# Seven-product multiplication inside eight of twelve units of a first product, fp16 operands, and a new order of the last products

## The chip, the cores and the metric

The kernel runs on one core of a Trainium2 chip. The core has five engines, each with its own queue of instructions: TensorE (PE, matrix products into PSUM), VectorE (DVE), ScalarE (ACT), GpSimd (POOL) and SyncE (SP, which here only issues transfers). The metric is the device time of one execution in microseconds. All times of the kernel before are three runs: 339.69, 339.77 and 337.69 us.

## The reference

```python
# q, k, v: (batch 8, heads 8, seq 576, head_dim 64); blocks of 64 positions
scores = scale * np.matmul(q, k.transpose(0, 1, 3, 2))
scores = np.where(block_i >= block_j, scores, -1000000000.0)      # causal by block
attn = softmax(scores)                                             # rows
x = np.matmul(attn, v)                    # -> (4608 rows, 512)
h = x @ w_in                              # (512, 2048)
g = h * (1.0 / (1.0 + np.exp(-beta * h)))
out = g @ w_out                           # (2048, 512)
```

Inputs and the output are float32. The kernel computes the swish as g = 0.5 h (1 + tanh(beta h / 2)); the 0.5 is applied where the output leaves PSUM.

## The kernel before

The attention goes over 32 pairs of heads (four per batch entry). Its result is written, turned, into xT, a ring of 2560 rows in SBUF. The two products of the feed-forward part go over nine chunks of 512 rows. A chunk's **first product** has 16 groups j of 128 features. A group is four products on PE (line 971, 512 columns each, contraction 4 x 128) into one PSUM bank, a tanh on ACT (line 981) that reads the bank, and a gate on DVE (line 985) that multiplies the bank by 1 + tanh into gT in fp16, after which the bank is free.

A chunk's **second product** (function `fast`, chunks 1 to 8) is already done by Strassen's seven products over halves of the rows, of the 2048 features and of the 512 outputs, in Winograd's form. Its combinations of gT are made on DVE by `comb` (line 856, two halves for each of four sums, partly in place in gT and partly in the spare tensor OV), those of w_out by `weights` (line 836). `prod` issues each of the seven products as two halves of eight matmuls with 256 columns (line 892). `evac` takes the banks out: on ACT without an addend (line 913), on DVE with one (line 916), `half` for half a bank (line 907), and `store` issues the output transfer (line 923), on ACT's queue, in the last chunk on SP's.

While the attention lasts, POOL casts the loaded Q, K and V (lines 657 and 568) into QKn and Vn, and SP issues loads and the transposes by transfer (lines 664 and 774). Banks 0 to 3 of PSUM belong to the attention's pairs of banks until the last pair has been given out; single banks come from 4 to 7 till then, and from all eight afterwards.

The order of every engine's instructions is fixed when the kernel is built. The class `Plan` holds all operations with a planned duration, dependences, buffers and a priority, and gives each engine, whenever it is free in planned time, the ready operation with the lowest priority number. On PE the first product's group j of chunk r has 1000 + 100 r + j, and the second product's halves get a place between the next chunk's groups. Planned durations are `mm(n)` for a matmul of n columns, `act_t` and `dve_t` for ACT and DVE:

```python
def mm(n):
    return max(n / 2.4 + 3, 55.0)
def act_t(n, ptr=0):
    return 0.833 * n + 93 + 93 * ptr
def dve_t(n):
    return (n + 125) / 0.96
```

The engines then follow their lists with semaphores; nothing in the plan stands for one engine's holding up of another at the SBUF.

Of the kernel before, what the change touches and what calls it, by code (L numbers as in the profile page):

```python
# [13 lines left out]
NF = 2048  # L14
# [17 lines left out]
class Op:  # L32
    def __init__(self, engs, dur, lat, emit, deps, tiles, prio, mode, dma, xfer):
        self.xfer = xfer
        self.engs, self.dur, self.lat, self.emit = engs, dur, lat, emit
        self.deps, self.tiles, self.prio, self.mode, self.dma = list(deps), tiles, prio, mode, dma
        self.eng = None
        self.start = self.end = None
        self.order = None
        self.need = False  # L40
        self.tick = None
        self.after = None
        self.lazy = False
        self.rest = 0.0
        self.pkt = 22.0
        self.fill = 0


class Plan:
# [35 lines left out]
    def schedule(self):  # L85
# [85 lines left out]
        while nsched < len(self.ops) - len(fill) or pend or rings["H"] or rings["S"] or late:  # L171
# [26 lines left out]
            while progress:  # L198
                progress = False
                for e in engs:  # L200
# [60 lines left out]
                    if e == "PE" and start < self.COLD:  # L261
                        o.lat += o.dur
                        o.dur *= 2
                    o.eng, o.start, o.end = e, start, start + o.lat
# [95 lines left out]
def bass_blockwise_causal_attn__then__act_swish_beta_kernel(  # L360
# [10 lines left out]
    with es:  # L371
# [10 lines left out]
        FAST = range(1, NRC)  # L382
        RX = 5 * RC
# [9 lines left out]
        QKn = [sb(f"QKn{i}", [128, 2, 2, 768], bf16) for i in range(NQ)]  # L393
        Vn = [sb(f"Vn{i}", [128, 5, 8, 66], bf16) for i in range(NQ)]
        QKT = [sb(f"QKT{i}", [128, 2, 2, 640], bf16) for i in range(3)]
        Ef = [sb(f"E{i}", [128, 3200], bf16) for i in range(NE)]
        gT = [sb(f"gT{i}", [128, NJ, RC], f16) for i in range(2)]

# [4 lines left out]
        xq = [sb(f"xq{i}", [128, 5, 128], bf16) for i in range(3)]  # L403
        xT = sb("xT", [128, 4, RX], bf16)
        identF = sb("identF", [128, 128], f32)
        identB = sb("identB", [128, 128], bf16)
        w_in = sb("w_in", [128, 4, NF], bf16)
# [7 lines left out]
        PSb = PS[:].rearrange("p b n -> p (b n)").bitcast(bf16).rearrange("p (b n) -> p b n", b=8)  # L415

        identW = identF[:].bitcast(bf16)
# [5 lines left out]
        P.slots("S4", 4)  # L423

# [105 lines left out]
        for b in range(B):  # L530
            ts, t = P.tile("Vs"), P.tile("V")
            ts.only = (b,) if b < 2 else (0,)
            early += [ts] * (b < 2)
            tl[b] = t
            for h0, h1, e, tt in PARTS[b]:

                vs = []
                for i in tt:
                    def fv(g, e, ts=ts, t=t, b=b, h0=h0, h1=h1, i=i):
                        d = Vn[t.slot] if e == "POOL" else Vs[ts.slot]  # L540
                        if i < 4:
                            return [g.dma_start(d[:, i, h0:h1, 0:64],
                                                v[b, h0:h1, 128 * i:128 * i + 128, :].rearrange("h p d -> p h d"))]
                        o = i - 4
                        return [g.dma_start(d[64 * o:64 * o + 64, 4, h0 + o:h1:2, 0:64],
                                            v[b, h0 + o:h1:2, 512:576, :].rearrange("h p d -> p h d"))]

                    n = (h1 - h0) / 8 * (1 if i < 4 else 0.25)
                    if e == "SP":
                        o = P.op("SP", 300 + 550 * n, fv, tiles=[ts], xfer=1400 * n,  # L550
                                 prio=3.5 + 0.1 * (h0 > 0) if b == 0 else 4 * b + (3.5 if b < 2 else 0.5),
                                 dma=["d_V", h0, 1])
                    else:
                        o = P.op("POOL", 150 + 1450 * n, fv, tiles=[t], xfer=1400 * n, prio=-30 if b == 0 else 4 * b + (3.5 if b < 2 else 0.5), dma=["d_VP", h0, 1])
                        o.after = lastv if b else None
                    vs.append(o)
                ld["V" if e == "SP" else "VP", b, h0] = vs
                if e == "POOL":
                    lastv = vs[-1]
                    for h in range(h0, h1, 2):  # L560
                        load.setdefault(4 * b + h // 2, []).extend([*vs, *ones, *vzero])
                    continue
                n = 5 if 4 in tt else len(tt)
                for g0 in range(h0, h1, 2):
                    g1 = g0 + 2

                    def fw(g, e, ts=ts, t=t, g0=g0, g1=g1, n=n):
                        return g.tensor_copy(Vn[t.slot][:, 0:n, g0:g1, 0:64], Vs[ts.slot][:, 0:n, g0:g1, :])  # L568

                    o = P.op("POOL", 60 + 60 * n * (g1 - g0), fw, deps=[*vs, *ones, *vzero], tiles=[ts, t],  # L570
                             prio=4 * b + 0.5 - (38.5 - 5 * (h0 > 0)) * (b < 1))
                    for h in range(g0, g1, 2):
                        load[4 * b + h // 2] = [o]
                lastv = o
# [20 lines left out]
        for u in range(NU):  # L595
# [3 lines left out]
            if p == 0:  # L599

                tn, tt_ = P.tile("QKn"), P.tile("QKT")
                turned = []
# [37 lines left out]
            elif p == 0:  # L640

                for w, (nm, src) in enumerate((("Q", q), ("K", k))):
                    ts = P.tile("S4")

# [197 lines left out]
        def fast(r, row, tg, gs):  # L842
# [17 lines left out]

            def piece(x, i):
                return x[:, SZ * i:SZ * i + SZ]

            for i in range(NP):
                SS[3].append(comb(lambda i=i: piece(SW[3], i), lambda i=i: G(0, 0, i), lambda i=i: G(1, 0, i), ALU.subtract, i,
                                  gs[SZ * i:SZ * i + SZ] + old, [tg, t3]))
            for i in range(NP):
                o = comb(lambda i=i: G(1, 0, i), lambda i=i: G(1, 0, i), lambda i=i: G(1, 1, i), ALU.add, i,
                         gs[SZ * i:SZ * i + SZ] + gs[HJ + SZ * i:HJ + SZ * i + SZ] + [SS[3][i]], [tg])
                o.same = gs[SZ * i:SZ * i + SZ] + gs[HJ + SZ * i:HJ + SZ * i + SZ]  # L870
                SS[3][i].same = gs[SZ * i:SZ * i + SZ]
# [12 lines left out]
            def prod(ps, fa, fb, deps, tiles, first, last):  # L884
                z = []
                pair = isinstance(ps, list)
                for w in range(2):
                    pw = ps[w] if pair else ps

                    def fp(g, e, w=w, pw=pw):  # L890
                        for j in range(HJ):
# [9 lines left out]
                                  prio=1000 + 100 * r + (16 + 0.1 * k if fin or k < 2 else 103 + 16 / 12 * (k - 2))))  # L901
# [20 lines left out]
            def store(to, a, b, x, after=None, rest=0.0, w=slice(0, 2)):  # L922
                o = P.op("SP" if fin else "ACT", 500, lambda g, e: [g.dma_start(  # L923
                    out_rows(a, b)[:, w], ost[to.slot][:].rearrange("p (w n) -> p w n", w=2)[:, w])],
                    deps=[x], tiles=[to], xfer=450 * (w.stop - w.start), dma=["d_ost", to], prio=-1)
                o.after, o.rest = None if fin else after, rest
                return o

            Z, W, Y = P.tile("P1"), P.tile("P1"), [P.tile("P1"), P.tile("P1")] if fin else P.tile("P1")
            oz, ou, ot, oc = (P.tile("ost") for _ in range(4))  # L930
            wl, wh = wout[0:2], wout[2:4]
            lo, hi = gs[0:HJ], gs[HJ:NJ]
# [15 lines left out]
            c22 = [half(Y[w], ot, p7 + [tt], ot, w) for w in range(2)] if fin else [evac(Y, ot, p7 + [tt], add=ot)]  # L948
# [3 lines left out]
            store(ot, 1, 1, c22[-1], after=c12)  # L952
            p4 = prod(Y, lambda: G(1, 1), lambda: TW[4], hi + tw[4] + c22, [], False, True)
            if fin:
                for w in range(2):
                    store(ou, 1, 0, half(Y[w], ou, [p4[w], u2], ou, w), w=slice(w, w + 1))
            else:
                store(ou, 1, 0, evac(Y, ou, p4 + [u2], add=ou), rest=1500.0 if r < NRC - 2 else 0.0)

        for r in range(NRC):  # L960
# [4 lines left out]
            gs, hs = [], []  # L965
            for j in range(NJ):
# [20 lines left out]
                gs.append(P.op("DVE", dve_t(512), fg, deps=[a] + (spare.users if r == 1 else []), tiles=[ph, tt, tg], prio=0))  # L987
# [10 lines left out]
            for w, d0, d1 in [(w, 0, DM) for w in range(4)]:  # L998
# [5 lines left out]
                for j0, j1 in parts:  # L1004
# [8 lines left out]
                    o = P.op("PE", n, fo, deps=gs[j0:j1] + wout[j0 // 4:(j1 + 3) // 4],  # L1013
# [87 lines left out]
```

## Time and profile before

The profiled execution took 338.08 us; the span from its first to its last instruction is 336.2 us.

| | busy us | share of the span |
|---|---|---|
| PE (matmuls) | 322.8 | 96% |
| DVE | 221.4 | 66% |
| ACT | 211.1 | 63% |
| POOL | 85.4 | 25% |

The timeline puts the chunks so: chunk 6's first tanh starts at 238.4 us, chunk 7's at 272.3, chunk 8's at 298.3, and its last one at 320.5. The attention's last product is at 260.9 us, the last POOL cast ends at 222.6, the last transpose of xT is issued at 263.5. The last matmul ends at 333.5.

In the lines of a profile, L971 is line 971 of the kernel. A group's line has the line, the engine, the operation, out<-in with the program's names, the shape, and how often; then busy us and mean ns of one, and the idle time of the engine just before. PEld is the load of PE's weights, which runs beside its products. A trace can miss some records of matmuls ("x19" for 20).

### The profile page before, as it was taken

To read this page: it belongs to the slowest core of one execution; us is meant where nothing else is said; L and a number is where in the kernel's file an instruction comes from. 1 tells how busy PE (TensorE), PEld (TensorE's weight loads), DVE (VectorE), ACT (ScalarE), POOL (GpSimd) and SP (SyncE) were. 2 spreads that over 40 slices of the span, in tenths; PEclk is the share of its full clock that TensorE was granted. 3 is DMA by queue.
4 is the path that set the end of the run, shared out by engine and by line. 5 is a ranking of instruction groups with operands and counts; after the bars stand their busy time and mean duration, and the time that the engine had idled before them with its cause. 6 is when DMAs were issued, how large, how long until landed. Compare 5 with 4: busy or idle time off the path is not lost.

```text
span 336.2 us, 7462 instructions
## 1 busy us (share of the span) xinstructions
PE 322.8 (96%) x3110; PEld 203.5 (61%) x3092; DVE 221.4 (66%) x449; ACT 211.1 (63%) x314; POOL 85.4 (25%) x127
## 2 busy tenths in 40 slices
PE   6799999999999999999999998999999999999996
PEld 4466456445577556655565675567556766666685
DVE  4548775669753788548974876578376866666742
ACT  2664975297556886577788557765777545544521
POOL 6747081073073044204420640420000000000000
PEclk9999999999999999999999999999999999999999
DMA  8999999999999999989699999985022201110023
GB/s 196 222 238 236 187 214 207 202 270 222 191 264 210 193 206 210 200 164 253 117 223 195 197 252 223 195 144 101 33 54 39 84 31 33 42 53 31 10 86 125
DMA packets 154993, 53.41 MB, mean 159 GB/s; under 512 B 139072, under 2 KB 154448, under 8 KB 154960
## 3 DMA queue, kind: packets, MB, share of 16 engines
q1 hardware_dynamic: 141200, 40.19, 64.3%
q0 software_dynamic: 5568, 4.36, 8.2%
q10 hardware_dynamic: 8192, 8.39, 7.6%
q8 instruction: 24, 0.39, 0.5%
q14 instruction: 9, 0.07, 0.1%
HBM read 36.71 MB, written 9.44 MB: 137 GB/s over the span
## 4 chain that ended last, share of the span: by engine, by line
PE 85%; DVE 5%; ACT 4%; DMA 2%; issue 1%; ACTq 1%; SPq 1%; POOL 0%; POOLq 0%
PE PS L971 34%; PE PS L892 27%; PE PS L748 8%; PE PS L696 8%; PE PS L1007 4%; ACT E L710 2%; DMA ST<-in_q_dram 2%; PE PS L519 2%; PE PS L787 1%; ACT th L981 1%; DVE xq L767 1%; PE PS L628 1%; DVE gT L985 1%; DVE gT L856 1%; ACTq L923 1%
## 5 line engine op out<-in xcount | busy, mean ns | idle before, releaser
L981 ACT ACTIVATE th<-PS,beta 128x512 f32<-128x512 f32 x144 | 96.5, 694 | 63.5 <-PE PS L971 61.5
L971 PE MATMUL PS<-xT,w_in 128*128 128x512 bf16 x538 | 129.7, 380 | 4.0 <-DVE E L718 1.0
L985 DVE SCALAR_TENSOR_TENSOR gT<-th,PS 128x512 f16<-128x512 f32 x144 | 95.8, 682 | 40.2 <-ACT th L981 39.6
L710 ACT ACTIVATE E<-PS 128x1024 bf16<-128x1024 f32 x93 | 91.8, 1025 | 25.5 <-PE PS L696 23.9
L971 PEld LDWEIGHTS PS<-xT,w_in 128*128 128x128 bf16 x576 | 52.5, 98 | 57.1 <-issue 3.4
L892 PE MATMUL PS<-w_out,gT 128*128 128x256 f16 x512 | 63.2, 273 | 0.2 <-DVE gT L985 0.2
L892 PEld LDWEIGHTS PS<-w_out,gT 128*128 128x128 f16 x512 | 48.8, 98 | 12.0 <-DVE gT L985 0.5
L657 POOL CAST QKn<-ST 128x640 bf16<-128x640 f32 x48 | 38.6, 805 | 28.7 <-DMA ST<-in_k_dram 17.4
L568 POOL CAST Vn<-Vs 128x640 bf16<-128x640 f32 (+1 forms) x28 | 20.4, 729 | 92.9 <-DMA Vs<-in_v_dram 91.7
L696 PE MATMUL PS<-QKT 64*128 64x512 bf16 (+4 forms) x328 | 37.1, 297 | 0.7 <-DVE xq L767 0.6
L748 PEld LDWEIGHTS PS<-Vn,E 128*128 128x128 bf16 x930 | 31.4, 97 | 4.5 <-DVE xq L767 0.6
L913 ACT ACTIVATE ost<-PS 128x512 f32<-128x512 f32 x32 | 19.2, 599 | 23.1 <-PE PS L892 23.0
L748 PE MATMUL PS<-Vn,E 128*128 128x65 bf16 x930 | 32.8, 193 | 0.6 <-DVE xq L767 0.5
L892 PE MATMUL PS<-OV 128*128 128x256 f16 x256 | 32.1, 273 | 0.0
L696 PEld LDWEIGHTS PS<-QKT 64*128 64x128 bf16 (+1 forms) x328 | 13.4, 96 | 27.5 <-issue 16.4
L892 PEld LDWEIGHTS PS<-OV 128*128 128x128 f16 x256 | 24.3, 98 | 6.2 <-issue 0.4
L767 DVE TENSOR_TENSOR xq<-PS,inv 128x640 bf16<-128x640 f32 x32 | 26.3, 821 | 0.6
L716 DVE MEMSET E<- 64x64 uint32 x62 | 6.9, 112 | 26.3 <-ACT E L710 24.3
L856 DVE TENSOR_TENSOR OV<-gT 128x1024 f16<-128x1024 f16 x32 | 23.2, 732 | 1.1 <-PE PS L892 0.6
L916 DVE SCALAR_TENSOR_TENSOR ost<-PS,ost 128x512 f32<-128x512 f32 x22 | 15.1, 685 | 5.6 <-PE PS L892 5.1
L892 PE MATMUL PS<-OV,gT 128*128 128x256 f16 x128 | 16.0, 273 | 0.0
L636 DVE COPY QKT<-PS 128x576 bf16<-128x576 bf16 x16 | 11.9, 755 | 5.6 <-PE PS L628 5.5
(61 smaller groups left out, 177.1 us busy)
## 6 DMA issues: line engine op xcount, KB each, us to landing
out_dram<-ost ACTq DMA_DIRECT2D x32, 256.0 KB, 3.4
ST<-in_q_dram SPq DMA_DIRECT2D x12, 576.0 KB, 6.1
ST<-in_k_dram SPq DMA_DIRECT2D x12, 576.0 KB, 8.0
Vs<-in_v_dram SPq DMA_DIRECT2D x24, 256.0 KB, 4.7
ST<-in_q_dram SPq DMA_DIRECT2D x8, 288.0 KB, 6.6
ST<-in_k_dram SPq DMA_DIRECT2D x8, 288.0 KB, 7.9
w_in<-in_moe_w_in_dram POOLq DMA_DIRECT2D x4, 512.0 KB, 11.0
w_out<-in_moe_w_out_dram POOLq DMA_DIRECT2D x4, 512.0 KB, 9.8
```

Of the source, the lines that this page charges most:

```text
L568: return g.tensor_copy(Vn[t.slot][:, 0:n, g0:g1, 0:64], Vs[ts.slot][:, 0:n, g0:g1, :])
L657: return g.tensor_copy(QKn[tn.slot][:].rearrange("p a w n -> p (a w n)")[:, 640 * (2 * a + w):][:, 0:640] .rearrange("p (t h d) -> p t h d ...
L696: z = g.matmul(o, QKT[tqk.slot][r, p, 1, 128 * t + y:128 * t + m + y], x)
L710: return g.activation(E3[es_(te)][:, g0, :, :], PS[:, ps.slot:ps.slot + 2, :], ACT.Exp, scale=0.125)
L748: z = g.matmul(o, eblk(te, t, i, h), Vn[Tv.slot][:, t, 2 * c + h, 0:65], start=(t == 0), stop=(t == i))
L767: return g.tensor_tensor(xq[tx.slot][:].rearrange("p i (h d) -> p h i d", h=2), both(pv, 0, 64), x, ALU.mult)
L856: return P.op("DVE", dve_t(SZ * HC / 2), mk(lambda g: g.tensor_tensor(fo(), fx(), fy(), op)), deps=deps, tiles=tiles, prio=prio)
L892: x = g.matmul(PS[:, pw.slot, HM * w:HM * w + HM], fa()[:, j, 128 * w:128 * w + 128], fb()[:, j, :], start=first and (pair or w == 0) and ...
L913: return P.op("ACT", act_t(DM) + 80, lambda g, e: g.activation(ost[to.slot][:], PS[:, ps.slot, :], ACT.Copy, scale=0.5), deps=deps, tiles= ...
L971: z = g.matmul(PS[:, ph.slot, :], w_in[:, c, 128 * j:128 * j + 128], xT[:, c, row % RX:row % RX + RC], start=(c == 0), stop=(c == 3))
L981: return g.activation(th[tt.slot][:], PS[:, ph.slot, :], ACT.Tanh, scale=beta[:, j:j + 1])
L985: return g.scalar_tensor_tensor(out=gT[tg.slot][:, j, :], in0=th[tt.slot][:], scalar=1.0, in1=PS[:, ph.slot, :], op0=ALU.add, op1=ALU.mult)
```

## The change

A **unit** m is four groups of the first product, 4m to 4m + 3, that is 512 features. In two units of chunk 6 and three units each of chunks 7 and 8 the product is done by seven products over halves of the 512 features, of the contraction and of the 512 rows (`inner`). Each of the seven is four matmuls of 256 columns. Two banks, Z and W, take turns: a product accumulates in its bank, ACT or DVE copies the partial result to SBUF (HT, fp32), or DVE adds it to one that lies there. Tanh and gates then read HT in place of PSUM. Of a unit's four gates two run on POOL, each as an addition and a multiplication. The sums of w_in (`inner_weights`, eight operations) are made on POOL once, in the buffers of the Q and K loads; the differences of xT are made on DVE for each chunk, in QKn's. HT lies in buffers of V and of QKT. The other groups of these chunks stay as they were.

Beside that: x, w_in, Q, K and their identity become fp16 in place of bf16; the slots of V and QKT are fixed by number; in the last chunk the seven second products come in another order (the seventh product ahead of the second, the third last, in two banks); chunk 7's stores move from ACT's queue to SP's; and in chunks 5 to 7 the second product's halves stand 1.1 apart in priority, not 1.33.

```diff
+        LATE2 = {NRC - 4: 1.1, NRC - 3: 1.1, NRC - 2: 1.1}
+        TSUM, TPR = ('DVE',), 0.4
+        BOTH1, ONPOOL = ("ACT", "DVE"), (0, 2)
+        FAST1 = {6: (0, 2), 7: (0, 1, 2), 8: (0, 1, 2)}
...
-        xT = sb("xT", [128, 4, RX], bf16)
+        xT = sb("xT", [128, 4, RX], f16)
...
-        w_in = sb("w_in", [128, 4, NF], bf16)
+        w_in = sb("w_in", [128, 4, NF], f16)
...
-                                  prio=1000 + 100 * r + (16 + 0.1 * k if fin or k < 2 else 103 + 16 / 12 * (k - 2))))
+                                  prio=1000 + 100 * r + (pos if fin else 16 + 0.1 * k if k < 2 else 103 + LATE2.get(r, 16 / 12) * (k - 2))))
...
-                o = P.op("SP" if fin else "ACT", 500, lambda g, e: [g.dma_start(
+                o = P.op("SP" if r >= NRC - 2 else "ACT", 500, lambda g, e: [g.dma_start(
...
+            if fin:
...
+                p1 = prod(Z, lambda: G(0, 0), lambda: quad(w_out, 0, 0), lo + wl, [], True, False, 16)
+                z1 = evac(Z, oz, p1)
+                p7 = prod(Y, lambda: SW[3], lambda: TW[3], SS[3] + tw[3], [t3], True, True, 16.1)
+                p2 = prod(W, lambda: G(0, 1), lambda: quad(w_out, 1, 0), hi + wh, [], True, True, 16.2)
...
+        def inner_weights():
+            old = [o for t in under["SI"] for o in t.users]
...
+                for n in range(2):
+                    z = P.op("POOL", 1900, mk(lambda g, o=o, x=x, y=y, n=n, op=op: g.tensor_tensor(
+                        o[:, n], x[:, n], y[:, n], op)), deps=old + win + [v[n] for q, v in si.items() if q < k], prio=40)
...
+        def inner(r, row, xd, tg, gs, hs, units):
...
+                t[k] = P.op(TSUM, dve_t(256), mk(lambda g, k=k, x=x, y=y: g.tensor_tensor(T(k), x(), y(), ALU.subtract)),
+                            deps=xd + oldT + [t[i] for i in same], tiles=[tx], prio=TPR)
...
+            for m in units:
+                ha, hb = P.tile("HT"), P.tile("HT")
+                Z, W = P.tile("P1"), P.tile("P1")
...
+                        for j in range(2):
+                            for c in range(2):
+                                z = g.matmul(PS[:, ps.slot, 256 * j:256 * j + 256], fa()[:, c, 128 * j:128 * j + 128],
+                                             fb()[:, c, :], start=first and j == 0 and c == 0,
+                                             stop=last and j == 1 and c == 1, skip_group_check=True)
...
+                             prio=1000 + 100 * r + 4 * m + 4 * k / 7)
...
+                p1 = prod(0, Z, lambda m=m: A(0, 0, m), lambda: X(0, 0), xd + win[m:m + 1], [ha, hb, tg, W], True, False)
+                c1 = copy(Z, ha, 0, [p1], BOTH1)
+                p2 = prod(1, W, lambda m=m: A(0, 1, m), lambda: X(1, 0), xd + win[m:m + 1], [], True, True)
+                h00 = add(W, ha, 0, [p2], c1)
+                p6 = prod(2, Z, lambda S=S: S(2), lambda: T(2), [c1, t[2], *si[2]], [tx], False, False)
+                c2 = copy(Z, hb, 0, [p6], BOTH1)
+                p7 = prod(3, W, lambda S=S: S(3), lambda: T(3), [h00, t[3], *si[3]], [tx], True, False)
+                p5 = prod(4, Z, lambda S=S: S(1), lambda: T(1), [c2, t[1], *si[1]], [tx], False, False)
+                c3 = copy(Z, hb, 1, [p5], BOTH1)
+                h11 = add(W, hb, 1, [p7], c3)
+                p3 = prod(5, Z, lambda S=S: S(4), lambda: X(1, 1), [c3, *si[4]], [], False, True)
+                h01 = copy(Z, ha, 1, [p3], BOTH1)
+                p4 = prod(6, W, lambda m=m: A(1, 1, m), lambda: T(4), [h11, t[4]], [tx], False, True)
+                h10 = add(W, hb, 0, [p4], c2)
...
+                        return g.activation(th[th_.slot][:], HT[tt_.slot][:, k], ACT.Tanh, scale=beta[:, j:j + 1])
...
+                        if e == "POOL":
+                            return g.tensor_tensor(gT[tg.slot][:, j, :], th[th_.slot][:], h, ALU.mult)
+                        return g.scalar_tensor_tensor(out=gT[tg.slot][:, j, :], in0=th[th_.slot][:], scalar=1.0,
+                                                      in1=h, op0=ALU.add, op1=ALU.mult)
...
+                    if j % 4 in ONPOOL:
+                        a = P.op("POOL", 650, mk(lambda g, th_=th_: g.tensor_scalar(
+                            out=th[th_.slot][:], in0=th[th_.slot][:], scalar1=1.0, scalar2=None, op0=ALU.add)),
+                            deps=[a], tiles=[th_], prio=0)
+                    o = P.op("POOL" if j % 4 in ONPOOL else "DVE", 1150 if j % 4 in ONPOOL else dve_t(512), fg,
+                             deps=[a, *deps], tiles=[th_, tt_, tg], prio=-0.1)
```

## The prediction

> **What bounds the kernel now.** I read four views, in this order. First the page's busy times and its chain of work that ended last.
>
> ```profile
> PE 322.8 (96%) x3110; PEld 203.5 (61%) x3092; DVE 221.4 (66%) x449; ACT 211.1 (63%) x314; POOL 85.4 (25%) x127
> ...
> PE 85%; DVE 5%; ACT 4%; DMA 2%; issue 1%; ACTq 1%; SPq 1%; POOL 0%; POOLq 0%
> ```
>
> TensorE (PE) is busy for 96% of the span and carries 85% of the chain. Second, the busy time of the engines in the stretches that the change touches: the attention's last block with chunk 6's first product, chunk 7's period, chunk 8's, the tail, and the stretch in which POOL falls idle. The first number after the window is its length, and then each engine's busy us follow.
>
> ```profile
> 236.40:266.00 29.60, 29.23 (x299) 18.33 (x297) 19.50 (x43) 22.23 (x33) 0.00 (x0) 1.00 0.18 42
> 266.00:292.20 26.20, 26.04 (x176) 17.27 (x177) 18.50 (x29) 13.41 (x21) 0.00 (x0) 1.00 0.12 41
> 292.20:318.30 26.10, 25.94 (x175) 17.18 (x176) 17.65 (x28) 13.40 (x21) 0.00 (x0) 1.00 0.12 41
> 318.30:336.20 17.90, 14.96 (x132) 12.56 (x130) 6.17 (x11) 3.55 (x6) 0.00 (x0) 1.00 0.31 104
> 222.00:240.00 18.00, 17.73 (x173) 11.58 (x169) 13.48 (x25) 11.03 (x16) 0.62 (x1) 1.00 0.50 99
> ```
>
> In chunks 7 and 8 PE idles for 0.16 us of 26, so it is work on PE, not a wait, that sets the end. DVE is at 18.5 of 26.2 us, ACT at 13.4, POOL at nothing. Third, the price of each kind of work, from the chain and the groups:
>
> ```profile
> 293.07 4.37 PE PS L892 x40
> 301.76 0.87 PE PS L892 x8
> 302.63 0.86 PE PS L971 x4
> ...
> 318.92 1.52 ACTq L923
> 321.95 11.54 PE PS L892 x104
> ```
>
> A product of 256 columns costs 4.37 / 40 = 109 ns, one of 512 columns 0.86 / 4 = 216 ns. The 1.52 us of the ACT queue before the last products is no stall of PE: the timeline there has PE idle only from 321.74 to 321.95, 0.2 us. Fourth, the groups of the engines that will get new work, and a collision. The groups:
>
> ```profile
> L981 ACT ACTIVATE th<-PS,beta 128x512 f32<-128x512 f32 x144 | 96.5, 694 | 63.5 <-PE PS L971 61.5
> L985 DVE SCALAR_TENSOR_TENSOR gT<-th,PS 128x512 f16<-128x512 f32 x144 | 95.8, 682 | 40.2 <-ACT th L981 39.6
> L657 POOL CAST QKn<-ST 128x640 bf16<-128x640 f32 x48 | 38.6, 805 | 28.7 <-DMA ST<-in_k_dram 17.4
> L913 ACT ACTIVATE ost<-PS 128x512 f32<-128x512 f32 x32 | 19.2, 599 | 23.1 <-PE PS L892 23.0
> ```
>
> The collision, from the timeline (start, length, then the instruction):
>
> ```profile
> 170.81 1.81 DVE L856 TENSOR_TENSOR gT<-gT,OV 128x1024 f16<-128x1024 f16 x2
> 170.88 2.32 POOL L657 CAST QKn<-ST 128x640 bf16<-128x640 f32 x2 [5.69 <-DMA ST<-in_k_dram]
> 221.12 1.50 POOL L657 CAST QKn<-ST 128x640 bf16<-128x640 f32 x2 [1.80 <-DMA ST<-in_k_dram]
> ```
>
> Two combinations (L856) need 1.28 us where POOL is idle and 1.81 us at 170.81, beside POOL casts; the casts need 1.50 us alone and 2.32 us there. The two engines hold each other up. After 222.6 us POOL never works again.
>
> **What the Trainium skill says.** "TensorE: Matmul & The Clock Gate", Back-to-back issue gap, gives N / 2.4 + 2.5 ns: 216 and 109 ns, as the trace has. "SBUF — State Buffer", Who interferes with whom, says that a DVE instruction with two SBUF inputs and a GpSimd one that reads SBUF exclude each other for a whole instruction; the pair above agrees. "GPSIMD Engine Reference", Elementwise, has tensor_tensor on fp32 at 4497 ns for 2048 elements, 2.2 ns each; no POOL tensor_tensor is in this trace. "VectorE: DVE Perf Modes", The TRN2 errata, has an fp32 tensor_tensor of 512 elements from SBUF at 691 ns; the trace has only the PSUM form, 682 ns.
>
> **The change, part by part.**
>
> PE. A unit is four groups of a chunk's first product. Now it is 16 products of 512 columns: 16 x 216 = 3.46 us. By seven products it is 7 x 4 = 28 of 256 columns: 28 x 109 = 3.06 us. Eight units (two in chunk 6, three in 7, three in 8) save 8 x 0.40 = **3.2 us** of PE, all on the path. The weights load in 98 ns (L892's PEld row) behind 109 ns, so nothing is exposed there. The last chunk's fourteen halves stay fourteen; their new order can win no more than the 0.2 us idle before them, and the tail after the last product (333.5 to 336.2: half an evacuation, a store) stays. Cost of the reordering and of the move of chunk 7's stores from ACT's queue to SP's: nothing, since SP has issued its last transpose at 263.5 and has only stores left; on ACT's queue each took 0.38 us. The fp16 types keep two bytes, hence the same rows.
>
> ACT and DVE, per unit. Added: four copies out of PSUM (0.60 each, L913's row; on ACT or DVE as the planner finds), three DVE additions with a PSUM input (0.685, L916's form). Four tanh stay, now from SBUF. Of four DVE gates (0.682) two stay, at 0.69, and two go to POOL. Per chunk come four differences of xT: half of L836's 1024 elements, 0.69 - 512/2/0.96 = 0.42 us each. In chunk 7's or 8's period with three units: ACT 13.4 + 12 x 0.60 = 20.6 us if it takes all copies; DVE 18.5 - 12 x 0.68 + 9 x 0.685 + 6 x 0.69 + 4 x 0.42 = 22.3 us. The period would be 26.2 - 1.2 = 25.0 us. Rows overstate what a queue needs: pairs of L985 follow one another at 0.60 us. With 30 such operations at 0.08 us less, DVE needs about 19.9 us. So neither is the bound by itself, but neither has room for long waits.
>
> POOL. Per unit two gates, each an addition and a multiplication of 512 elements. The addition: between casts of 256 elements (408 ns) and 640 (720 ns) lies 0.62 us. The multiplication: at the page's 2.2 ns it is 1.12 us; from below 0.62 us, since it does no less than the addition, from above twice that, 1.24 us, were both inputs read one after the other. I take 1.12. Three units: 6 x 1.74 = 10.4 us of 25. POOL's gates are 1 us later than DVE's; the plain groups 12 to 15 and the previous chunk's products lie between them and their readers. Without those the last unit would cost that 1 us.
>
> The lock. In a period DVE runs 8 combinations, 6 gates from SBUF and 4 differences: 18 with two SBUF inputs. POOL is busy 10.4 / 25 = 0.42 of the time, and what is left of its operation then is (0.62^2 + 1.12^2) / (2 x 1.74) = 0.47 us on the mean: 18 x 0.42 x 0.47 = 3.6 us of DVE waiting a period. DVE is then at 23.5 of 25. Behind a held DVE operation stand the additions that free the banks W, and PE's fifth and seventh product of the unit wait for those; PE's order is fixed, so all after them wait too. In 160 to 200 us a dozen such collisions left PE idle 0.26 us in all, so most is absorbed; a unit's chain (product, copy, product, four times over in bank Z: 4 x (0.44 + 0.2 + 0.6) = 5 us for 3.06 us of products) has less slack. Bounds: 0 and all of 2 x 3.6 us. I take a fifth: **+1.4 us**.
>
> The weights' sums. Eight POOL operations of 1024 elements: 2.2 ns gives 2.25 us each; from below the cast's 0.81 ns per element, 1.0 us. I take 2.25: 18 us, from 222.6 to about 241. They are hidden as POOL's work, but each holds the lock. Against them run five combinations (223.8 to 234.7 in the timeline) and chunk 6's four differences after 234.5, when the last transpose that it needs has landed. Lone ones wait 1.1 us; those that follow one another wait for a whole POOL operation each: some 3 x 1.1 + 4 x 2 = 11 us of DVE waiting where DVE idles 4.5 of 18 us. Attention still holds half the banks then, so late gates hold PE. Bounds: 0 and the 6.5 us that don't fit. I take **+1.2 us**. With a POOL operation of 1.0 us it is nothing.
>
> Sum against the profiled execution (span 336.2 us, time 338.08, 1.9 us around it): -3.2 - 0.2 + 1.4 + 1.2 = -0.8 us, 337.3 us. That execution lies 1.6 us below the median of the three runs, 339.69 us; taken from there it is **338.9 us**. The three runs lie 0.6% apart, so 1% is about what this kernel can tell from no change.
>
> **Rivals.**
>
> *All of the gain* (0.13). The locks are absorbed as in 160 to 200 us: -3.2, -0.2, and up to 0.3 us of small gaps: 336.0 us, just past 1%. For it speaks how little of a collision reached PE there; against it the chains and DVE at 94%.
>
> *DVE becomes the bound in chunks 6 to 8* (0.28). If half of the copies go to DVE, it needs 19.9 + 3.6 + 3.6 = 27.1 us in a period of 25.0: 2.1 us too much, twice, and 3 us around the weights' sums: -3.4 + 4.2 + 3 = +3.8 us, 343.5 us, slower than before. It decides from the point where DVE's own work and its lock waits pass 25.0 us, that is from three copies a period on DVE. For it speaks that POOL's holding is in no planned duration; against it that the planned 0.66 us per DVE operation exceeds the 0.60 us which the timeline shows.
>
> *PE doesn't save what it should* (0.04): four-product instructions with a wait each, in place of runs of eight; with 50 ns for each of 56, 2.8 us of the 3.2 go: 341.7 us.
>
> The forecast, partly eaten gain, has 0.55: from 336.4 to 341.5 us.
>
> **How the numbers follow.** Faster by over 1% (below 336.3 us): the first rival, 0.13. Slower by over 1% (above 343.1 us): most of the second, 0.23, and what both bounds give at their worst, 0.05: 0.28. Within 1%: the rest, 0.59. The range leaves a tenth out on each side: 336.0 below, since no more than the whole gain can come; above, the second rival with a little more waiting, 344.2 us.
>
> **What would show it.** Right: L971's count falls by 128, 224 products of 256 columns come with 109 ns each, PE's busy time between 236 and 318 us is 3.2 us lower; combinations and gates with two SBUF inputs of over 1 us beside POOL; PE gaps after 222 us of some 3 us, with DVE as releaser. Wrong: POOL's multiplication far from 1.1 us, PE gaps below 1 us (the first rival) or DVE over 95% busy from 266 to 318 us (the second), or gaps that ACT's tanh and copies release, which I have as harmless.

## The result, and the profile after

The changed kernel takes 351.57 us (median of 4 runs, 351.14 to 351.96) where the kernel before takes 338.69 in the same comparison: a ratio of 1.0388, 95% interval 1.0327 to 1.0449. That is 13 us slower. (Here and below a median is of all executions, while a ratio compares only those within 1.5% of the fastest of their kernel, so the two can differ by 1 us.) The forecast was 338.9 us with a range up to 344.2; even the rival on the slower side, 343.5 us, is 8 us short of it.

The profiled execution took 351.14 us, with a span of 349.3. From the page, the busy times of the engines and the chain's shares:

```profile
PE 326.3 (93%) x3244; PEld 212.7 (61%) x3188; DVE 254.7 (73%) x481; ACT 221.4 (63%) x334; POOL 151.0 (43%) x167
PE 66%; DVE 11%; POOL 11%; ACT 5%; issue 3%; DMA 2%; SPq 1%; ACTq 0%; POOLq 0%; DVEq 0%
```

PE's share of the chain fell from 85% to 66%. What took its place is POOL, from nothing to 11% (38 us), and DVE, from 5% to 11%. (The sums of PE busy time can't be compared directly: the trace of before has 538 of the 576 matmuls of L971.) The busy time by engine (PE, PEld, DVE, ACT, POOL) in the last block of the attention and in two later stretches, the first number after the window being its length, and the three last PE's mean granted clock, the share of time in which the DMA engines work, and GB/s:

```profile
222.00:240.00 18.00, 15.84 (x158) 10.54 (x154) 15.03 (x22) 9.97 (x14) 17.30 (x9) 1.00 0.38 85
266.00:292.00 26.00, 24.54 (x222) 19.33 (x220) 23.30 (x39) 13.96 (x24) 8.90 (x7) 1.00 0.13 38
292.00:320.00 28.00, 24.93 (x211) 20.02 (x208) 24.80 (x35) 18.25 (x30) 19.38 (x13) 1.00 0.14 48
```

PE, which idled 0.16 us of 26, now idles 1.5 us of 26 and 3.1 us of 28, and 2.2 us of the first 18, where POOL makes the sums of w_in. From 222 us to its last matmul PE idles 11.5 us, against 1.1 us before. The other 2.5 us of the loss in this execution lie before 222 us, ahead of the first unit (the same second product starts at 221.66 us where it started at 219.15 before); the last section comes back to them. The groups of the new work, and of the combinations beside it (shapes kept apart; busy us, mean ns of one, then idle before):

```profile
L1127 POOL TENSOR_SCALAR th<-th 128x512 f32<-128x512 f32 x16 | 26.3, 1642 | 44.5 <-ACT th L1114 43.4
L880 DVE TENSOR_TENSOR OV<-gT 128x1024 f16<-128x1024 f16 x32 | 31.2, 979 | 3.8 <-POOL gT L1122 2.2
L1122 POOL TENSOR_TENSOR gT<-th,Vs 128x512 f16<-128x512 f32 x8 | 10.6, 1328 | 0.7
L1023 POOL TENSOR_TENSOR ST<-w_in 128x1024 f16<-128x1024 f16 x4 | 9.1, 2287 | 0.3
L1123 DVE SCALAR_TENSOR_TENSOR gT<-th,QKT 128x512 f16<-128x512 f32 x4 | 4.8, 1200 | 0.2 <-ACT th L1114 0.2
```

The POOL addition (L1127) takes 1642 ns on the mean, where the forecast had 620. The multiplication (L1122) takes 1328 against 1120, the sum (L1023) 2287 against 2250. DVE's gate from SBUF (L1123) takes 1200 in the slowest of its groups, against 690. And PE waits for POOL: in the answer on waits from 266 to 336 us (waiting instruction, releaser: us in all, times, longest)

```profile
ACT th L1114 <- POOL gT L1122: 5.0, 4, 1.6
PE PS L1061 <- POOL gT L1122: 4.5, 3, 1.7
DVE OV L880 <- POOL gT L1122: 2.2, 2, 1.2
```

The forecast had a POOL gate 1 us late, with no one waiting for it. The chain between 304 and 313 us (start, length, what) shows how it runs instead:

```profile
304.52 0.73 ACT th L1114
305.33 1.50 POOL th L1127
306.91 1.67 POOL gT L1122
308.73 1.75 POOL th L1127
310.54 1.28 POOL gT L1122
311.85 0.70 DVE gT L880
```

Two gates on POOL take 6.5 us end to end, about twice a unit's 3.06 us of products, and the chain doesn't leave POOL in between. A combination on DVE (L880) waits for the last of them.

Last, five of the six combinations that DVE runs while POOL makes the sums (timeline of DVE: start, length, instruction):

```profile
224.48 1.86 DVE L880 TENSOR_TENSOR OV<-gT 128x1024 f16<-128x1024 f16 x1 [0.56 <-PE PS L919]
226.99 1.88 DVE L880 TENSOR_TENSOR OV<-gT 128x1024 f16<-128x1024 f16 x1
232.34 1.72 DVE L880 TENSOR_TENSOR OV<-gT 128x1024 f16<-128x1024 f16 x1
239.00 2.00 DVE L880 TENSOR_TENSOR gT<-gT 128x1024 f16<-128x1024 f16 x1
241.03 2.49 DVE L880 TENSOR_TENSOR OV<-gT 128x1024 f16<-128x1024 f16 x1
```

Alone each takes 0.69 us; here they take 9.95 us in place of 3.45. From 238.32 POOL's timeline has two sums in 4.65 us, so one ends near 240.65 and the other at 242.97; the two last combinations end at 241.00 and 243.52, each 0.35 to 0.55 us after a sum. A combination that begins while a sum runs ends only after that sum. The sixth, at 230.83 us, began just before a sum ended (two run from 228.40 us in 5.11 us) and took 0.69. Behind the two last ones (and a difference of xT) an evacuation of a bank (L943) waits its turn on DVE, and behind that PE, until 244.51:

```profile
244.51 1.92 PE L919 MATMUL PS<-w_out,gT 128*128 128x256 f16 x16 [1.99 <-DVE ost L943]
```

### The profile page after: what moved, and what is told of

Same layout as the page of the kernel before. It is cut to its first block, busy times and chain, and to the rows that moved or that the text cites. A ratio compares the mean times of both kernels' runs of the same rounds, so it can differ in the third digit from the quotient of the medians.

```text
span 349.3 us, 7804 instructions
## 1 busy us (share of the span) xinstructions
PE 326.3 (93%) x3244; PEld 212.7 (61%) x3188; DVE 254.7 (73%) x481; ACT 221.4 (63%) x334; POOL 151.0 (43%) x167
## 4 chain that ended last, share of the span: by engine, by line
PE 66%; DVE 11%; POOL 11%; ACT 5%; issue 3%; DMA 2%; SPq 1%; ACTq 0%; POOLq 0%; DVEq 0%
PE PS L1149 24%; PE PS L919 18%; PE PS L720 7%; PE PS L772 7%; POOL th L1127 6%; POOL gT L1122 5%; PE PS L1185 4%; PE PS L1061 2%; DVE OV L880 2%; DVE gT L1163 2%; DMA ST<-in_k_dram 2%; ACT E L734 2%; DVE gT L880 1%; PE PS L537 1%; PE PS L811 1%
## 5 line engine op out<-in xcount | busy, mean ns | idle before, releaser
L1149 PE MATMUL PS<-xT,w_in 128*128 128x512 f16 x448 | 107.9, 382 | 4.0 <-issue 2.9
L1159 ACT ACTIVATE th<-PS,beta 128x512 f32<-128x512 f32 x112 | 74.8, 695 | 46.2 <-PE PS L1149 42.3
L1163 DVE SCALAR_TENSOR_TENSOR gT<-th,PS 128x512 f16<-128x512 f32 x112 | 73.8, 680 | 23.0 <-ACT th L1159 22.6
L1149 PEld LDWEIGHTS PS<-xT,w_in 128*128 128x128 f16 x448 | 40.7, 98 | 48.4 <-issue 6.0
L681 POOL CAST QKn<-ST 128x640 f16<-128x640 f32 x48 | 37.9, 790 | 30.4 <-DMA ST<-in_k_dram 22.3
L1127 POOL TENSOR_SCALAR th<-th 128x512 f32<-128x512 f32 x16 | 26.3, 1642 | 44.5 <-ACT th L1114 43.4
L720 PE MATMUL PS<-QKT 64*128 64x320 f16 (+4 forms) x328 | 37.4, 299 | 1.3 <-DVE xq L791 1.1
L880 DVE TENSOR_TENSOR OV<-gT 128x1024 f16<-128x1024 f16 x32 | 31.2, 979 | 3.8 <-POOL gT L1122 2.2
L720 PEld LDWEIGHTS PS<-QKT 64*128 64x128 f16 (+1 forms) x328 | 13.4, 96 | 28.8 <-issue 15.7
L791 DVE TENSOR_TENSOR xq<-PS,inv 128x640 f16<-128x640 f32 x32 | 26.3, 821 | 0.6
L943 DVE SCALAR_TENSOR_TENSOR ost<-PS,ost 128x512 f32<-128x512 f32 x25 | 17.2, 687 | 5.6 <-ACT ost L940 2.7
```

The costliest lines, as they stand in the source:

```text
L681: return g.tensor_copy(QKn[tn.slot][:].rearrange("p a w n -> p (a w n)")[:, 640 * (2 * a + w):][:, 0:640] .rearrange("p (t h d) -> p t h d ...
L720: z = g.matmul(o, QKT[tqk.slot][r, p, 1, 128 * t + y:128 * t + m + y], x)
L791: return g.tensor_tensor(xq[tx.slot][:].rearrange("p i (h d) -> p h i d", h=2), both(pv, 0, 64), x, ALU.mult)
L880: return P.op("DVE", dve_t(SZ * HC / 2), mk(lambda g: g.tensor_tensor(fo(), fx(), fy(), op)), deps=deps, tiles=tiles, prio=prio)
L1127: a = P.op("POOL", 650, mk(lambda g, th_=th_: g.tensor_scalar(out=th[th_.slot][:], in0=th[th_.slot][:], scalar1=1.0, scalar2=None, op0=ALU ...
L1149: z = g.matmul(PS[:, ph.slot, :], w_in[:, c, 128 * j:128 * j + 128], xT[:, c, row % RX:row % RX + RC], start=(c == 0), stop=(c == 3))
```

## The experiments

Six candidates stood for the loss: the types, slots and new order, apart from the units; the **sums on POOL**, by holding up DVE at the SBUF; the same sums, by the products that wait for them; **POOL's gates**, by holding up DVE; POOL's gates, by coming late; and DVE and ACT at their limit with the units' copies and additions, whatever POOL does. (That POOL and DVE hold each other up is called the lock in the prediction and below, and the shared port in the expectations.) The kernel before has medians of 337.06 to 337.4 us in the three comparisons below, each on another chip; differences in us are differences of ratios times 337.

**The units left out.**

```diff
-        FAST1 = {6: (0, 2), 7: (0, 1, 2), 8: (0, 1, 2)}
+        FAST1 = {}
```

> The changed kernel with no unit at all: the first product of chunks 6 to 8 stays as it was before, and with it go the weights' sums, the differences, the copies and POOL's gates. Types, fixed slots, the order of the last products, the stores of chunk 7 and the spacing of 1.1 stay changed. Theory A (POOL's gates are too slow) and theory B (POOL's weights' sums hold DVE) and theory D (copies and additions saturate DVE and ACT) all lie in the units: 338 to 339 us, a ratio of 0.995 to 1.005. Theory C (something outside the units, such as PE's 2.9 us wait at 203 us with the lower clock after it): 342 us or more, ratio over 1.01.

Measured: 337.32 us, ratio 0.9989 [0.9965, 1.0013]. The fp16 types, the fixed slots, the order of the last products, the stores on SP's queue and the spacing of the halves cost nothing that shows together (the interval goes from -1.2 to +0.4 us), as forecast. The loss is in the units.

**POOL's operations cut short.** In the first kernel the two POOL operations of a gate run over 64 of 512 columns; in the second the sums of w_in over 64 of 1024, and the products read w_in itself in their place; in the third both. The other columns are left out. Order and dependences of the gates stay.

```diff
-        out=th[th_.slot][:], in0=th[th_.slot][:], scalar1=1.0, ...
+        out=th[th_.slot][:, 0:64], in0=th[th_.slot][:, 0:64], scalar1=1.0, ...
...
-        g.tensor_tensor(gT[tg.slot][:, j, :], th[th_.slot][:], h, ALU.mult)
+        g.tensor_tensor(gT[tg.slot][:, j, 0:64], th[th_.slot][:, 0:64], h[:, 0:64], ALU.mult)
```

```diff
-        o[:, n], x[:, n], y[:, n], op)
+        o[:, n, 0:1, 0:64], x[:, n, 0:1, 0:64], y[:, n, 0:1, 0:64], op)
...
-                S = lambda k, m=m: SI[k - 1][:, :, m, :]
+                S = lambda k, m=m: A(0, 0, m)
```

Gates short:

> The changed kernel in its own order on every engine, but POOL's addition and multiplication for a gate work on 64 of 512 columns (the other columns of these gates are left out). POOL then holds neither the gates nor the shared port. A: most of the loss from 239 us on goes, some 8 of the 13 us: 343 us, ratio 1.014. B: 350 us, ratio 1.034, with the loss before 240 us untouched. D: 349 us.

Sums short:

> The changed kernel in its own order, but the eight sums of w_in on POOL are made for 64 of 1024 columns, and the products read w_in itself in their place (so their values are left out, their number and size not). POOL is then free from 224 to 243 us. B: the 2.5 us lost between 222 and 240 us and what follows from them go: 347 us or less, ratio 1.025. A: at most 2 us go, 349.5 us, ratio 1.032.

Both short:

> Both cuts together, the changed kernel's order kept: POOL does next to nothing after 224 us. A with B: the saving of PE shows, less what the wait at 203 us costs: 338 to 340 us, ratio 1.00. D: DVE and ACT stay the bound in chunks 6 to 8: 345 us or more, ratio 1.02, with DVE over 90% busy from 280 to 332 us.

| | median us | ratio | 95% interval |
|---|---|---|---|
| gates short | 342.53 | 1.0141 | 1.0070 to 1.0211 |
| sums short | 342.73 | 1.0139 | 1.0058 to 1.0220 |
| both short | 334.27 | 0.9931 | 0.9907 to 0.9955 |

With both short the kernel is 0.0069 x 337 = 2.3 us faster than before (3.1 us by the medians), and the windows of its PE are full, though DVE is as busy as in the changed kernel and ACT busier:

```profile
266.00:292.00 26.00, 26.00 (x225) 21.78 (x224) 24.61 (x44) 18.12 (x32) 5.98 (x12) 1.00 0.07 22
292.00:320.00 28.00, 28.00 (x244) 23.57 (x242) 24.54 (x40) 19.49 (x32) 5.46 (x14) 1.00 0.20 67
```

So PE's saving is real, and the copies, additions and differences fit beside it. This rules out DVE and ACT at their limit as the cause of the loss. Against this kernel the full sums cost 0.0210 x 337 = **7.1 us**, and the full gates 0.0208 x 337 = **7.0 us**, each known to within 2.5 to 3 us. With the gain the account reads -2.3 + 7.1 + 7.0 = +11.8 us, where the change measures 0.0388 x 337 = 13.1; these intervals cover the rest.

Where each cost lies shows in the windows. Gates short:

```profile
222.00:240.00 18.00, 15.62 (x152) 10.03 (x144) 16.63 (x21) 9.57 (x13) 17.36 (x9) 1.00 0.37 85
240.00:266.00 26.00, 23.00 (x248) 15.60 (x243) 19.95 (x40) 16.09 (x27) 3.36 (x5) 0.93 0.16 41
```

Sums short:

```profile
222.00:240.00 18.00, 18.00 (x167) 12.67 (x159) 15.14 (x30) 11.73 (x17) 1.75 (x6) 1.00 0.50 93
266.00:292.00 26.00, 21.53 (x175) 16.39 (x174) 23.03 (x33) 13.38 (x24) 15.81 (x11) 1.00 0.06 21
```

The sums open 2.4 us of gaps before 240 us and 3.0 after, and the clock column (0.93) shows another 0.07 x 26 = 1.8 us: 7.2 us in all. (In the changed kernel's own profile, which came 2.5 us late into this stretch, the gap behind the combinations is 1.99 us, and the clock stays at 1.00.) The gates open 4.5 us in one period, with PE full while the sums would run.

**Sums that nobody reads.** The sums run in full on POOL; the products read w_in in their place and wait for none of them (`ghost` marks operations for which nobody waits).

```diff
+                    z.ghost = True
...
-                S = lambda k, m=m: SI[k - 1][:, :, m, :]
+                S = lambda k, m=m: A(0, 0, m)
...
+        for o in P.ops:
+            o.deps = [d for d in o.deps if o.ghost or not d.ghost]
```

> The changed kernel in its own order with POOL's sums of w_in at full length, but no product waits for them: the products read w_in itself in their place (values left out). POOL's gates are as in the changed kernel. If the sums cost time by holding the shared port against DVE, nothing is won: 350 to 352 us, as the changed kernel. If they cost time by products that wait for the sums: 343 us, as with the short sums.

Measured: 350.31 us, 1.0376 [1.0319, 1.0433], the change's own time. So the sums cost by being executed beside DVE, not by being waited for. Nor do POOL's gates queue behind them: here POOL idles 12.86 us between its last sum and its first gate. The timeline of DVE (lines here stand one or two later), and PE's first instruction after it:

```profile
235.44 2.49 DVE L881 TENSOR_TENSOR OV<-gT 128x1024 f16<-128x1024 f16 x1
237.86 2.33 DVE L1049 TENSOR_TENSOR QKn<-xT 128x512 f16<-128x512 f16 x1
240.11 0.68 DVE L944 SCALAR_TENSOR_TENSOR ost<-PS,ost 128x512 f32<-128x512 f32 x1
```

```profile
240.85 2.45 PE L920 MATMUL PS<-w_out,gT 128*128 128x256 f16 x14 [3.91 <-DVE ost L944]
```

A combination takes 2.49 us in place of 0.69 and a difference of xT 2.33 in place of 0.42. The evacuation L944 reads PSUM and is itself not slowed; it stands behind them on DVE, it frees the bank, and PE waits 3.91 us for it.

**POOL's gates: lateness and the lock apart.** Both kernels have the short sums. In the first, POOL's gates run in full and at their place, but on a buffer and w_in's bits, and nobody waits for them. In the second everyone waits as in the change, but POOL's operations are memsets of about the same length, which read nothing.

```diff
-        out=th[th_.slot][:], in0=th[th_.slot][:], scalar1=1.0, ...
+        out=dum, in0=wf, scalar1=1.0, ...
...
-        g.tensor_tensor(gT[tg.slot][:, j, :], th[th_.slot][:], h, ALU.mult)
+        g.tensor_tensor(dum2, dum, wf, ALU.mult)
...
+            o.deps = [d for d in o.deps if o.ghost or not d.ghost]
```

> On the base of the short sums (342.7 us; with short gates too 334.3 us): POOL's additions and multiplications run at full length in the same places, but on a buffer that nobody reads, so that no tanh, copy, combination or product waits for them; two gates of each unit are left out. What stays is that they hold the shared port against DVE. If the port is the gates' cost: 341 to 343 us. If waiting for late gates is the cost: 335 to 337 us.

```diff
-        g.tensor_scalar(out=th[th_.slot][:], in0=th[th_.slot][:], ...)
+        (g.memset(dum[:, 0:1024], 1.0), g.memset(th[th_.slot][:], 1.0))
...
-        g.tensor_tensor(gT[tg.slot][:, j, :], th[th_.slot][:], h, ALU.mult)
+        g.memset(dum[:, 0:820], 1.0)
+        g.memset(gT[tg.slot][:, j, :], 0.5)
```

> On the base of the short sums: POOL's addition and multiplication are each replaced by two memsets that together take about as long (1024 and 512 columns, 820 and 512), so that the gates are as late as before and hold their buffers as long, but POOL reads nothing from SBUF; the gates' values are left out. If the port is the gates' cost: 334 to 336 us. If waiting for late gates is the cost: 340 to 343 us.

Measured: 340.07 us, 1.0082 [1.0056, 1.0109], with nobody waiting; 339.10 us, 1.0056 [1.0029, 1.0083], with memsets. I had expected that one of the two would cost nearly all and the other nearly nothing. It is neither. Against both-short (0.9931) the lock alone costs 0.0151 x 337 = **5.1 us** and lateness alone 0.0125 x 337 = **4.2 us**, each to within 1.2 us; the memsets are a little shorter than the operations that they stand for (1.48 and 1.31 us, against 1.64 and 1.33). Together the gates cost 7.0 us. That this is less than the sum would fit a wait for the one covering part of the other, but the interval of the 7.0 is too wide to show it. That the two mechanisms were kept apart shows in the DVE groups from 244 us on. First nobody waiting, then memsets:

```profile
L884 DVE TENSOR_TENSOR gT<-gT,OV 128x1024 f16<-128x1024 f16 x6 | 7.0, 1194 | 0.0
L1127 DVE SCALAR_TENSOR_TENSOR gT<-th,Vn 128x512 f16<-128x512 f32 x4 | 4.9, 1219 | 0.9 <-ACT th L1118 0.8
```

```profile
L881 DVE TENSOR_TENSOR gT<-gT,OV 128x1024 f16<-128x1024 f16 x6 | 3.9, 683 | 0.0
L1125 DVE SCALAR_TENSOR_TENSOR gT<-th,Vn 128x512 f16<-128x512 f32 x4 | 2.8, 690 | 2.0 <-ACT th L1115 1.9
```

These are the groups that were held most. They fall from 1194 and 1219 ns to 683 and 690, their time alone, where POOL reads nothing. And in the memset kernel's waits from 266 to 336 us POOL still releases what it held:

```profile
ACT th L1115 <- POOL gT L1124: 3.9, 4, 1.4
PE PS L1062 <- POOL gT L1124: 2.7, 3, 1.0
```

**The change planned with the measured durations.** POOL's three operations get their measured times in the plan, and the order is made anew.

```diff
-                        a = P.op("POOL", 650, ...
+                        a = P.op("POOL", 1640, ...
...
-  ... 1150 if j % 4 in ONPOOL else dve_t(512), fg,
+  ... 1320 if j % 4 in ONPOOL else dve_t(512), fg,
...
-                    z = P.op("POOL", 1900, ...
+                    z = P.op("POOL", 2350, ...
```

> The change as it is, but planned with POOL's durations as the trace of the changed kernel has them: 1640 ns for the addition (650 before), 1320 for the multiplication (1150), 2350 for a sum (1900). The order of all engines is then made for the late gates; the holding of the port stays unplanned. If the wrong prices are most of the cause: 342 us or less. If the port is: it stays within 3 us of the changed kernel, 348 us or more, since the sums hold DVE as before.

Measured: 348.20 us, 1.0335 [1.0280, 1.0389]. By the ratios 0.0053 x 337 = 1.8 us of the 13 come from an order made for too short POOL operations, and the intervals overlap. The new order does relieve the gates (PE idles 1.6 us from 266 to 320 us, where the changed kernel idles 4.5), but the plan has no lock in it, and a PE gap of 3.90 us, behind an evacuation on DVE, is again there, from 238.6 to 242.5 us.

**Only the sums moved to DVE**, eight units and POOL's gates kept, with a new order:

```diff
-                    z = P.op("POOL", 1900, mk(...
+                    z = P.op("DVE", dve_t(512), mk(...
+                    z.same = [v[n] for q, v in si.items() if q < k]
```

> The change with one part undone: the eight sums of w_in on DVE (0.69 us each) and not on POOL, planned anew; eight units, POOL's gates as in the change. If the sums on POOL cost 8 us by holding DVE, this takes nearly all of it away: 343 to 345 us, ratio 1.02, the rest being POOL's gates. If DVE has no room for 5.5 us more, 347 us or more.

Measured: 348.06 us, 1.0359 [1.0290, 1.0428], a miss: I had expected the sums' cost to go. PE is busy for 18.00 of 18.00 us from 222 to 240, so that stall is gone; but after 270 us gaps of 1.36, 2.18, 1.58, 1.22 and 2.14 us stand in this kernel's PE timeline, the first ended by a gate on DVE and the four others by POOL's multiplication. Its order is another one, so this is no clean undoing of one part; why the gates cost it more than they cost the sums-short kernel (342.73 us) stays open.

**Nothing on POOL.** Sums and gates on DVE, with eight, five and four units:

```diff
-        BOTH1, ONPOOL = ("ACT", "DVE"), (0, 2)
+        BOTH1, ONPOOL = ("ACT", "DVE"), ()
...
-        FAST1 = {6: (0, 2), 7: (0, 1, 2), 8: (0, 1, 2)}
+        FAST1 = {7: (0, 1, 2), 8: (0, 1)}      # five; four: {7: (0, 1), 8: (0, 1)}
...
-                    z = P.op("POOL", 1900, mk(...
+                    z = P.op("DVE", dve_t(512), mk(...
```

> All eight units, sums and all gates on DVE, nothing on POOL, planned anew. If POOL is the only cause, the saving of 3.2 us shows: 334 to 335 us, ratio 0.991. If DVE and ACT are the next bound once POOL carries nothing (my rival of the prediction), 340 us or more, ratio above 1.01, with DVE over 90% busy in chunk 7's and 8's periods and PE gaps released by DVE or ACT.

> A version of the change without POOL: the eight sums of w_in and all gates on DVE, five units (three in chunk 7, two in chunk 8, none in chunk 6), planned anew. If POOL was the whole cause, PE's saving of 5 x 0.40 = 2.0 us shows against 337.3 us without units: 335.3 us, ratio 0.994. If DVE, which gets 5.5 us of sums and ten gates from SBUF more, is the next bound: 338 us or more, ratio above 1.00.

> As the version with five units and no POOL (335.3 us, ratio 0.992), but four units, two in chunk 7 and two in chunk 8. If PE's saving per unit is what counts: 337.3 - 4 x 0.40 = 335.7 us, ratio 0.995. If the second unit of a chunk is already one too many for DVE: above 336.5 us.

| units | median us | ratio | 95% interval |
|---|---|---|---|
| eight | 343.09 | 1.0170 | 1.0104 to 1.0237 |
| five | 335.34 | 0.9921 | 0.9894 to 0.9949 |
| four | 335.80 | 0.9945 | 0.9921 to 0.9968 |

With five units the kernel is 0.0079 x 337 = 2.7 us faster than the kernel before, and faster than the changed one too; four units give 1.9 us. (By the medians it is 1.7 and 1.3 us.) At 0.40 us of PE a unit, 2.0 and 1.6 us were to be had, within the intervals. In the five-unit kernel PE is full and DVE is not:

```profile
266.00:292.00 26.00, 26.00 (x214) 20.73 (x213) 23.31 (x42) 17.11 (x29) 0.00 (x0) 1.00 0.17 49
292.00:320.00 28.00, 28.00 (x228) 22.04 (x226) 25.87 (x43) 19.87 (x33) 0.00 (x0) 1.00 0.17 58
```

With all eight on DVE, PE falls behind again:

```profile
266.00:292.00 26.00, 23.75 (x206) 17.36 (x203) 24.62 (x45) 17.68 (x30) 0.00 (x0) 1.00 0.06 17
```

DVE is at 95% there, but that alone shows no limit: with both short it is as busy (24.61 us), and PE is full. The waits do show it. PE has four gaps of over 0.5 us from 266 us on; two are ended by gates on DVE (1.06 and 2.30 us), one by an addition on DVE (0.57) and one by a copy on ACT (0.62). So the recorded rival "DVE becomes the bound" is a limit of this design, met when POOL takes no share. These 4.6 us are not all of the 0.0239 x 337 = 8.1 us to both-short; the rest was not taken apart. The limit is not what made the change slow.

## Why the prediction failed

The sum had -3.2 - 0.2 for PE, +1.2 for the weights' sums and +1.4 for POOL's gates, -0.8 us in all. The runs show -2.3, +7.1 and +7.0. So both terms for POOL failed: 5.9 and 5.6 us are missing there.

**PE's saving: right.** Eight units with short POOL operations show -2.3 us by the ratios, -3.1 by the medians, against -3.2; four and five units agree within their intervals. L971's count fell by 128 as forecast (576 to 448), and 224 products of 256 columns came.

**Types, queues and reordering at nothing: right** as far as 1 us can be told, by the kernel without units.

**"The addition: between casts of 256 elements (408 ns) and 640 (720 ns) lies 0.62 us": the first step that failed.** It measures 1.49 us at the least and 1.64 on the mean. The casts are another operation, and I took their interpolation as the value with no upper end, although the same paragraph bounds the multiplication from both sides. A POOL gate is then 1.64 + 1.33 = 2.97 us, not 1.74, and three units a period take 6 x 2.97 = 17.8 us, not 10.4.

**"POOL's gates are 1 us later than DVE's; the plain groups 12 to 15 ... lie between them and their readers": failed.** The readers of gT had less slack than that: combinations (L880) waited for POOL's gates for 2.2 us and 0.9 us, and a second product for 0.9. And a gate also holds th, of which there are three buffers, and HT, of which there are four. ACT's next tanh needs the one, the first product of a later unit needs the other: these are the two largest waits quoted above, 5.0 and 4.5 us. The two gates of one unit end 6.5 us after the first one's tanh lets them start. Lateness alone measures 4.2 us, where the sum had nothing. The step looked only for the readers of the output, gave them too much slack, and left out the buffers that the operation keeps busy.

**The lock of the gates: the right mechanism, with its waiting and its way to PE both mis-sized.** The sum had 2 x 3.6 us of DVE waiting and took a fifth, 1.4 us; alone it measures 5.1. The waiting can be read off the DVE groups from 244 us on: the same 48 combinations, gates from SBUF and differences take 41.8 us where nobody waits for the gates, and 30.1 us beside memsets, so DVE waits 11.7 us, chunk 6's units included. Of these 5.1 / 11.7 = 0.44 reached the end, not 0.2. With the measured durations the prediction's own formula gives a busy share of 17.8 / 26 = 0.68, a rest of (1.64^2 + 1.33^2) / (2 x 2.97) = 0.75 us, and 18 x 0.68 x 0.75 = 9.2 us a period; that is 18.4 us in two periods, more than the trace has. So the short addition had hidden that the formula itself overstates.

**The lock of the sums: the waiting sized in the right order, its way to PE not.** The sum had some 11 us of DVE waiting, +1.2 us taken, 6.5 us as the bound. The five combinations alone waited 9.95 - 3.45 = 6.5 us. The cost measures 7.1 us, at the bound and not at a fifth of it, because PE's share of it isn't limited to the DVE time that doesn't fit: one evacuation behind a held combination stops PE for 3.91 us even though DVE has idle time elsewhere, and PE's clock falls after such a gap (1.8 us), for which the sum had no term.

**"In 160 to 200 us a dozen such collisions left PE idle 0.26 us in all, so most is absorbed": the inference behind both small fractions, failed.** Nor was DVE held a dozen times there: the trace before has it held in three places (0.83 us for a combination at 162.25, 1.81 for the two at 170.81, 0.91 at 190.43), for 0.9 us in all; elsewhere it was the casts that waited. There POOL's operations are casts of 0.72 us that come and go. Here they are 1.3 to 2.5 us each and follow one another, so that a two-input operation on DVE can wait for most of one. The waits of up to 0.5 us there left PE almost full; two of 1.3 and 1.8 us in a row, the change's two last combinations, did not.

**The rivals.** "All of the gain" would have needed POOL's work at no cost; its own sum, -3.2 - 0.2 + 0.3 from 339.69, gives 336.6 us, not 336.0. "DVE becomes the bound" has 343.5 us, and eight units without POOL take 343.1; that the two are so near is luck, since the rival's sum has 3.6 us of lock waits in each period and 3 us around the weights' sums, and with nothing on POOL that kernel has none of these. The change reached 351 us by another way. No rival had POOL's own chain of gates as the wait.

## What to carry to other kernels

Price an operation given to an idle engine by the same operation on that engine, and where no row has it, leave the range open upward: here the value taken from the nearest rows was short by a factor of 2.6. Follow not only who reads its output but every buffer it keeps while it runs. Two-input work on GpSimd beside a busy VectorE was paid twice here, by coming late (4.2 us) and by holding VectorE up (5.1 us). With all of it on VectorE and five units the kernel was faster than before and after, by 2.7 us against before.

## What was not expected of the hardware

- A POOL addition of a constant on fp32 (128x512, in place) takes 1.49 us at the least, more than the multiplication of two inputs (1.27 to 1.33) and twice a cast of 640 elements (0.72). Cut to 64 columns it still takes 0.50 us.
- A POOL memset doesn't hold up DVE: the gates and combinations of the two groups above take 690 and 683 ns, where POOL operations that read SBUF make them 1219 and 1194. The Trainium skill, "SBUF — State Buffer", Who interferes with whom, says the same: a DVE instruction with two SBUF inputs contends with a GpSimd one that reads SBUF, not with one that only writes it. How long such a hold lasts it doesn't say for this pair; here the combinations ended 0.35 to 0.55 us after a POOL sum.
- After the gap of 3.9 us PE's mean clock over the next 26 us was 0.93 in three kernels (gates short, sums unread, and the measured durations). In the gates-short kernel, cut finer, it is 0.50 from 244 to 246 us and 1.00 again from 247. The Trainium skill, "TensorE: Matmul & The Clock Gate", Part 1, has the clock at half after an idle window of some 3.4 us, in windows that run freely. The half agrees. The length doesn't explain all: after the gap of 2.92 us near 203 us in the changed kernel's profile the clock was 0.50 too, from 207 to 209 us, after one of 2.18 us in the kernel with the sums on DVE it was 0.54 from 288 to 290, and after gaps of 2.1 and 2.3 us near 203 us in two others (the measured durations, four units) it stayed at 1.00.
- PE's wait before a group of chunk 5's first product near 203 us differs between profiles: 2.92 us in the changed kernel's, with a clock of 0.92 from 200 to 222 us, 2.52 in the five-unit kernel's, 0.40 with both short, whose order is the changed kernel's. It accounts for the 2.5 us before 222 us named above. A transpose into xT was issued at 202.23 us, 4.2 us before PE went on, so a late transpose is likely; what sets it was not tried.
